# Score sessions of four key-major blocks, PV per 512 queries and V for four head groups at a time, in two sliding-window attention layers

## The chip, the cores and the metric

One core of one Trainium2 chip (not the same chip in every job). The metric is the device time of one execution in microseconds (us); medians of several executions are given with their range. PE is the TensorE matmul engine, DVE is VectorE, ACT is ScalarE, POOL is GpSimd, SP is SyncE, which issues DMAs. The profile comes from one execution; its span is 1 to 2 us shorter than the time of that execution. "Granted clock" is the share of full speed that TensorE was given; in this case's traces it is 1.00 or 0.5, in steps of 3.4 us.

## The reference

Two independent layers A and B, outputs put side by side. Each has 2048 tokens, width 1024, 32 heads of 32 dimensions, and a causal window of 256 keys:

```python
qkv = (x @ wqkv).reshape(B, S, 3, H, Dh)...          # S = 2048, H = 32, Dh = 32
scores = einsum("bhqd,bhkd->bhqk", q, k) * Dh ** -0.5
mask = (i - j >= 0) & (i - j < 256)
p = softmax(where(mask, scores, -1e9))
out = einsum("bhqk,bhkd->bhqd", p, v)...reshape(B, S, D) @ wo
```

In blocks of 128, a query block meets three key blocks, so a head has 45 blocks of scores (16 + 15 + 14). Four heads form a group; two layers of eight groups make 16 groups.

## The kernel before

Matmuls of the projections fill the time in which TensorE would wait for exponentials: a "session" is the scores of one query block, their exp, and then some filler. The tiles that decide what may run ahead:

```python
ps_st   = tile_pool(name="ps_st",   bufs=1, space=PSUM)   # scores st [P, 4, 512] F32
ps_acc  = tile_pool(name="ps_acc",  bufs=1, space=PSUM)   # acc [P, 2, 2, 128] F32: PV | row sums, 256 queries
ps_proj = tile_pool(name="ps_proj", bufs=3, space=PSUM)   # pp, of every projection
```

For each query block i, up to three blocks of scores for each of four heads, and one exp over all of them:

```python
st = ps_st.tile([P, 4, 512], F32, name="st")
for jj in range(nk):                                      # nk = 1, 2, 3, 3, ...
    for r in range(4):                                    # four heads
        nc.tensor.matmul(st[:, r, jj*P:(jj+1)*P], lhsT=kT[...], rhs=qT[..., i*P:(i+1)*P],
                         start=True, stop=True, tile_position=(32*r, 0))
nc.scalar.activation(out=pt[:, :, kb0:kb0+nk, a, :], in_=st[...], func=ACT.Exp, ...)
```

Two query blocks later comes PV (the exponentials times V) with the row sums in the same accumulator, then on DVE two reciprocals and one multiplication into oT. The filler of a group is Q and K (64 matmuls of 512 columns) and V (128 of 128 columns, four blocks in one pp buffer), in the order in which the sessions need them, the same amount in every group:

```python
for g in range(G):
    for i in range(NB):
        emit_proj(inf, g, i // 4)                         # what this session cannot do without
        pt = qk_exp_mask(g, i)
        if i % 2 == 1 and len(pend) >= 2: pvl_pair(*pend.pop(0))
        ...
        emit_proj(max(need_p, budget - need_o), g + 1)    # filler, then the output projection of A
```

Each finished Q or K chunk is cast out of pp by DVE (an eviction: it frees the pp buffer; V and the output are evicted by ACT), which then takes its absolute maximum for a certificate that exp without a running maximum is safe (a slow path exists and is not taken). The certificate's last step is one tiny matmul at the end.

## Time and profile before

| | before |
|---|---|
| time | 664.51 us median of 3 (663.87 to 665.25) |
| PE, DVE, ACT busy | 94%, 67%, 63% of the span |
| chain that ended last | PE 89%, DVE 4%, ACT 2% |
| granted clock | 1.00 until the last slice (no record before 13.9 us) |

The prediction quotes the page's shares and waits. Two more rows of the page: busy tenths of PE, and granted clock, in 40 equal slices (9 is 90% or more). And one group: its columns are line, engine, operation, output and input, count, then busy us and mean ns of one, then idle time before it.

```profile
PE   4999999999999999999999999999999999999996
PEclk9999999999999999999999999999999999999998
...
L260 DVE RECIPROCAL rinv<-acc 128x128 f32<-128x128 f32 x256 | 226.3, 925 | 112.4 <-PE acc L251 111.5
```

There is no slice in which TensorE rests. The reciprocal is DVE's largest group: 256 of 0.925 us.

### The profile page before, as it was taken

Reading aid. Unit: us, or ns where it says so; the run is one execution under the profiler, and the core shown is the slowest. Engines: PE = TensorE matmul, PEld = TensorE weight load, DVE = VectorE, ACT = ScalarE, POOL = GpSimd, SP = SyncE. Lnnn points to the kernel's source line nnn. Section 1 sums busy time; section 2 is a strip of 40 time slices with the busy share of each in tenths; the row PEclk is TensorE's granted clock in tenths of the full one; section 3 lists DMA queues with packets and bytes.
Section 4 is the critical chain, followed back from the end, with each engine's and each line's share of the span. In section 5 each row is a group of like instructions: output and inputs, shape, how many; then the busy total and the mean of one; then the engine's idle time right before and its main releaser. Section 6 shows DMA issues by size and latency. Waiting matters only on the chain.

```text
span 663.4 us, 22408 instructions
## 1 busy us (share of the span) xinstructions
PE 626.1 (94%) x10175; PEld 366.6 (55%) x10308; DVE 444.7 (67%) x677; ACT 418.8 (63%) x385; POOL 294.3 (44%) x487
## 2 busy tenths in 40 slices
PE   4999999999999999999999999999999999999996
PEld 2555666665565655565555555555555555544442
DVE  1688877878788888877676777767676777553000
ACT  0666666576676676667666667666666667775332
POOL 0454545455455555555545455444545445452000
PEclk9999999999999999999999999999999999999998
DMA  9992202022010116102020020202011000011121
GB/s 209 278 253 43 49 2 49 4 48 44 9 42 9 32 28 136 38 3 49 18 65 2 20 64 2 66 18 49 19 31 37 18 2 18 34 49 54 75 80 68
DMA packets 89733, 35.06 MB, mean 53 GB/s; under 512 B 83488, under 2 KB 83488, under 8 KB 89632
## 3 DMA queue, kind: packets, MB, share of 16 engines
q1 hardware_dynamic: 89632, 33.56, 20.7%
q8 instruction: 82, 1.34, 0.9%
q14 instruction: 19, 0.16, 0.1%
HBM read 16.78 MB, written 8.39 MB: 38 GB/s over the span
## 4 chain that ended last, share of the span: by engine, by line
PE 89%; DVE 4%; issue 2%; ACT 2%; SPq 1%; DMA 1%; ACTq 0%; DVEq 0%
PE pp L133 33%; PE pp L151 18%; PE pp L193 16%; PE acc L251 13%; PE st L216 10%; ACT pt L224 2%; DVE rinv L260 2%; DVE pm L139 1%; SPq L82 1%; DMA wst<-in_A_wqkv_dram 1%; DVE oT L261 0%; DVE kT L110 0%; ACT osb L108 0%; DVE qT L110 0%; ACT vt L108 0%
## 5 line engine op out<-in xcount | busy, mean ns | idle before, releaser
L224 ACT ACTIVATE pt<-st 128x1536 bf16<-128x1536 f32 (+2 forms) x256 | 350.9, 1371 | 172.1 <-PE st L216 170.2
L260 DVE RECIPROCAL rinv<-acc 128x128 f32<-128x128 f32 x256 | 226.3, 925 | 112.4 <-PE acc L251 111.5
L228 POOL TENSOR_SCALAR_AFFINE_SELECT pt<-pt 128x512 bf16<-128x512 bf16 x256 | 162.4, 634 | 309.9 <-ACT pt L224 309.9
L133 PE MATMUL pp<-xT,wst 128*128 128x512 bf16 x912 | 234.8, 383 | 20.6 <-issue 10.0
L133 PEld LDWEIGHTS <-wst 128*128 128x128 bf16 x1024 | 87.0, 98 | 102.8 <-issue 14.4
L232 POOL TENSOR_SCALAR_AFFINE_SELECT pt<-pt 128x512 bf16<-128x512 bf16 x224 | 142.1, 634 | 0.0
L151 PE MATMUL pp<-wst,xT 128*128 128x128 bf16 x2048 | 140.4, 220 | 0.7 <-issue 0.5
L151 PEld LDWEIGHTS <-xT 128*128 128x128 bf16 x2048 | 119.6, 98 | 24.1 <-issue 7.4
L193 PE MATMUL pp<-wo_sb,oT 128*128 128x512 bf16 x491 | 127.6, 379 | 3.1 <-issue 1.3
L216 PEld LDWEIGHTS <-kT 32*128 32x128 bf16 x2880 | 44.5, 92 | 94.2 <-issue 89.0
L216 PE MATMUL st<-qT,kT 32*128 32x128 bf16 x2880 | 86.7, 218 | 4.7 <-ACT pt L224 3.6
L193 PEld LDWEIGHTS <-oT 128*128 128x128 bf16 x512 | 47.3, 98 | 50.5 <-issue 1.3
L110 DVE CAST qT<-pp 128x512 bf16<-128x512 f32 x64 | 43.3, 677 | 41.0 <-PE pp L133 37.2
L108 ACT CAST osb<-pp 128x512 bf16<-128x512 f32 x64 | 37.4, 585 | 47.7 <-PE pp L193 46.8
L251 PE MATMUL acc<-pt,vt 128*32 128x256 bf16 (+1 forms) x1920 | 63.3, 249 | 1.9 <-DVE oT L261 1.7
L251 PE MATMUL acc<-pt,ones 128*32 128x256 bf16 (+1 forms) x1920 | 62.3, 246 | 0.0
L261 DVE TENSOR_TENSOR oT<-acc,rinv 128x256 bf16<-128x256 f32 x128 | 53.6, 419 | 2.9
L108 ACT CAST vt<-pp 128x512 bf16<-128x512 f32 x64 | 37.2, 582 | 18.1 <-PE pp L151 17.9
L139 DVE TENSOR_REDUCE pm<-qT 128x1 f32<-128x512 bf16 x64 | 43.8, 684 | 1.7
L139 DVE TENSOR_REDUCE pm<-kT 128x1 f32<-128x512 bf16 x64 | 43.6, 681 | 1.2
L110 DVE CAST kT<-pp 128x512 bf16<-128x512 f32 x64 | 42.2, 660 | 2.6 <-PE pp L133 2.1
L251 PEld LDWEIGHTS <-vt 128*32 128x32 bf16 x1920 | 33.8, 95 | 17.4 <-DVE oT L261 3.4
(20 smaller groups left out, 48.2 us busy)
## 6 DMA issues: line engine op xcount, KB each, us to landing
out_dram<-osb SPq DMA_DIRECT2D x32, 256.0 KB, 2.0
wst<-in_A_wqkv_dram SPq DMA_DIRECT2D x24, 256.0 KB, 4.2
wst<-in_B_wqkv_dram SPq DMA_DIRECT2D x24, 256.0 KB, 4.3
wo_sb<-in_A_wo_dram SPq DMA_DIRECT2D x1, 2048.0 KB, 8.8
wo_sb<-in_B_wo_dram SPq DMA_DIRECT2D x1, 2048.0 KB, 11.0
xT<-in_A_x_dram SPq DMA_TRANSPOSE x4, 7.4
xT<-in_B_x_dram SPq DMA_TRANSPOSE x4, 7.3
```

The costliest lines, as they stand in the source:

```text
L108: nc.scalar.copy(out=out, in_=in_)
L110: nc.vector.tensor_copy(out=out, in_=in_)
L133: nc.tensor.matmul(st_["pp"][:], lhsT=wst[g][:, ct, which, :], rhs=xt[:, ct, o:o + QW], start=(ct == 0), stop=(ct == CT - 1))
L139: nc.vector.tensor_reduce(out=grp[g][3][:, which, sc:sc + 1], in_=dst, axis=AX.X, op=ALU.max, apply_absolute_value=True)
L151: nc.tensor.matmul(st_["pv"][:, a, :], lhsT=xt[:, ct, o:o + P], rhs=wst[g][:, ct, 2, :], start=(ct == 0), stop=(ct == CT - 1))
L193: nc.tensor.matmul(st_["po"][:], lhsT=oTs[pi * T + ct][:, sb * P:(sb + 1) * P], rhs=wo_sb[pi][:, ct, ch * cfg.NW:(ch + 1) * cfg.NW], start ...
L216: nc.tensor.matmul(st[:, r, jj * P:(jj + 1) * P], lhsT=kT[32 * r:32 * r + 32, (j0 + jj) * P:(j0 + jj + 1) * P], rhs=qT[32 * r:32 * r + 32, ...
L224: nc.scalar.activation(out=pt[:, :, kb0:kb0 + nk, a, :], in_=st[:, :, :nk * P].rearrange("p r (j q) -> p r j q", q=P), func=ACT.Exp, bias= ...
L228: nc.gpsimd.affine_select(out=dg, in_=dg, pattern=[[0, 4], [1, P]], compare_op=ALU.is_ge, fill=0.0, base=0, channel_multiplier=-1)
L232: nc.gpsimd.affine_select(out=fb, in_=fb, pattern=[[0, 4], [-1, P]], compare_op=ALU.is_gt, fill=0.0, base=0, channel_multiplier=1)
L251: nc.tensor.matmul(acc[32 * r:32 * r + 32, which, a0:a0 + na, :], lhsT=lhsT, rhs=pt[:, r, kb, a0:a0 + na, :], start=(which == 0 and n == 0 ...
L260: nc.vector.reciprocal(out=rinv[:, a, :], in_=acc[:, 1, a, :])
```

## The change

The intent is fewer and larger pieces: less change between kinds of matmul, fewer instructions, a cheaper certificate, no rest of projection work at the end.

1. **Key-major sessions.** The 45 (key block, query block) pairs are listed key by key and cut into sessions of four: 12 per group instead of 16. One score matmul takes all queries that belong to one key block.
2. **PV per 512 queries**: acc grows to two banks' worth, so pp goes from three buffers to two. Reciprocals and multiplications are queued and issued between filler matmuls.
3. **V for four groups at a time**, 512 columns wide: V is wanted every fourth group only.
4. Filler is a list of chains (matmuls that fill one pp buffer) with earliest and latest sessions, and a session emits the larger of a base and of what the deadlines need.
5. The certificate becomes an in-place OR over the bit patterns; the head loads smaller pieces on two queues and warms TensorE with zero matmuls; the output projection starts right behind the last group.

A session that finds no filler to emit is called dry below.

```diff
+QB = 4
+SLOTS = 4
+NS_BASE = 1750.0
+PV_LAG = 2
...
-    ps_proj = ctx.enter_context(tc.tile_pool(name="ps_proj", bufs=3, space=PSUM))
+    ps_proj = ctx.enter_context(tc.tile_pool(name="ps_proj", bufs=2, space=PSUM))
...
-                        evac(EVAC_QK, dst, st_["pp"][:])
-                        nc.vector.tensor_reduce(out=grp[g][3][:, which, sc:sc + 1], in_=dst,
-                                                axis=AX.X, op=ALU.max, apply_absolute_value=True)
+                    nc.vector.tensor_copy(out=dst, in_=st_["pp"][:])
+                    seen = top[:, which, :].bitcast(I32)
+                    nc.vector.tensor_tensor(out=seen, in0=seen, in1=dst.bitcast(I32),
+                                            op=ALU.bitwise_or)
...
+    for m in range(NPROB * T // SB):                      # SB = 4 groups
+        for b in range(NB):
+            k = b // QB
+            g = m * SB
+            early = NS * (g - 1) if k < 2 else pv_time(g - 1, k - 1) + 1
+            chains.append(_Chain(early, pv_time(g, k), v_steps(m, b)))
...
+    def need(now):
+        rate, work = 0.0, sum(ns for ns, _ in current)
+        for c in chains:
+            if c.late >= 10 ** 6:
+                break
+            work += NS_MM * CT
+            rate = max(rate, work / (c.late - now)) if c.late > now else rate
+        return rate
...
+            for _, f in qk_steps(0, which, 0, lo, hi, held[which], last=(hi == 512)):
...
+        emit(now, max(NS_BASE, need(now)))
```

## The prediction

> **What bounds the kernel now.** I read the engine shares first, then the chain of work that ended last, then the waits, then a stretch of the timeline. From the page, busy time by engine and the chain by engine and by line:
>
> ```profile
> PE 626.1 (94%) x10175; PEld 366.6 (55%) x10308; DVE 444.7 (67%) x677; ACT 418.8 (63%) x385; POOL 294.3 (44%) x487
> ...
> PE 89%; DVE 4%; issue 2%; ACT 2%; SPq 1%; DMA 1%; ACTq 0%; DVEq 0%
> PE pp L133 33%; PE pp L151 18%; PE pp L193 16%; PE acc L251 13%; PE st L216 10%; ACT pt L224 2%; DVE rinv L260 2%; DVE pm L139 1%; SPq L82 1%; DMA wst<-in_A_wqkv_dram 1%; DVE oT L261 0%; DVE kT L110 0%; ACT osb L108 0%; DVE qT L110 0%; ACT vt L108 0%
> ```
>
> TensorE is the bound: 89% of the chain, and all of it in five kinds of matmul: Q/K projection (L133), V projection (L151), output projection (L193), PV with row sums (L251), scores (L216). ACT is 63% busy and DVE 67%, so neither is near its limit on average. The waits say how rarely PE is held up by them (engine and line, released by: us in all, times, longest):
>
> ```profile
> PE st L216 <- ACT pt L224: 3.6, 10, 0.6
> PE acc L251 <- DVE oT L261: 1.7, 4, 0.5
> PE pp L193 <- ACT osb L108: 1.2, 3, 0.4
> ```
>
> That is 6.5 us of 663. Busy time of single matmuls overlaps, so I take PE's cost from start-to-start times in the timeline (start, length, what):
>
> ```profile
> 241.00 2.12 PE L133 MATMUL pp<-xT,wst 128*128 128x512 bf16 x9
> 243.04 0.35 PE L216 MATMUL st<-qT,kT 32*128 32x128 bf16 x12
> 243.32 0.51 PE L251 MATMUL acc<-pt,vt 128*32 128x128 bf16 x16
> 243.66 0.50 PE L251 MATMUL acc<-pt,ones 128*32 128x128 bf16 x16
> ...
> 253.41 1.35 PE L151 MATMUL pp<-wst,xT 128*128 128x128 bf16 x21
> 254.69 0.35 PE L216 MATMUL st<-qT,kT 32*128 32x128 bf16 x12
> ```
>
> Nine 512-wide matmuls and the step into the scores take 2.04 us: 9 x 0.2157 = 1.94, and 0.10 of change. Twelve score matmuls hold PE 0.28 us; elsewhere x8 holds it 0.22 and x4 0.17, so 0.055 us per block of 4 heads and 0.115 fixed. The 16 PV matmuls take 0.34 us: 6 blocks at 0.0556. V's 128-wide matmuls follow each other in 0.056. From the end of row sums to the next full matmul is 0.10.
>
> Sum for before: 1536 wide matmuls x 0.2157 = 331.3; 2048 V x 0.056 = 114.7; scores 16 groups x (16 sessions x 0.215 + 45 blocks x 0.0556) = 95.1; PV 16 x (8 x 0.10 + 90 x 0.0556) = 92.9. That is 634.0. The head is 8.6 us to the first matmul plus 3.4 for 16 matmuls at 0.43 instead of 0.216; the tail after the last projection 6.6; waits about 9. Total 661.6 against the 663.4 profiled. The sum closes, so I trust its terms.
>
> **What the Trainium skill says.** "TensorE: Matmul & The Clock Gate", section "Wait — 56ns, not 53.3ns?", gives 55.6 and 215.7 ns start to start at N = 128 and 512; the trace agrees (0.056, 0.2157). So V in 512-wide matmuls gains only the fixed 2.5 ns per matmul, not a factor. "TensorEngine Tiling (Array Packing)", "Key Properties", says that changing the tiling mode drains TensorE; the trace shows 0.10 to 0.115 us per change. "ScalarE: Activation LUTs", "What ACT_TABLE_LOAD costs", gives an ACTIVATE with immediates as 186 ns + 0.833 ns per element. The exps of three widths agree (us busy, mean ns of one):
>
> ```profile
> L224 ACT ACTIVATE pt<-st 128x1536 bf16<-128x1536 f32 x224 | 324.9, 1450 | 150.2 <-PE st L216 148.3 <-PE pp L151 1.2
> ...
> L224 ACT ACTIVATE pt<-st 128x1024 bf16<-128x1024 f32 x16 | 16.4, 1025 | 12.1 <-PE st L216 12.1
> ...
> L224 ACT ACTIVATE pt<-st 128x512 bf16<-128x512 f32 x16 | 9.6, 598 | 9.7 <-PE st L216 9.7
> ```
>
> Slope (1450 - 598) / 1024 = 0.832; 2048 elements should take 1.876 us. The first page's "What's actually happening" says idle TensorE falls to half clock after some 3.4 us windows; before shows 1.00 from stage to stage, so no run tests it yet.
>
> **The change part by part.** Scores: 12 sessions per group in place of 16 (45 blocks, four to a session, one in the last). 16 x (12 x 0.215 + 45 x 0.0556) = 81.3, saves 13.8. PV: four per group instead of eight, same columns: 16 x (4 x 0.10 + 90 x 0.0556) = 86.5, saves 6.4. V: 512 wide matmuls x 0.2157 = 110.4, saves 4.3. Q/K and output projection keep their 1536. PE's work falls by 24.5 to 609.5 us. Exps: 176 of 1.876 and 16 of 0.598 are 339.8 us, against 350.9: ACT gains little. DVE: casts and reciprocals stay; 128 reductions of 0.68 (87 us) become in-place ORs over 256 words; DVE is no bound. POOL's 480 selects stay.
>
> Head: weights go on ACT's queue instead of behind a 4.1 us transpose issue, the first x piece is half as long, zero matmuls warm the clock. I estimate the first real matmul at 7.5 us, at full clock, but then the second x piece is wanted at about 11 and, 4.1 us of issue plus about 7.4 us to landing behind it, comes at 12 to 14: 2.5 us of wait. Head 10 instead of 12. Tail about 6, as the certificate is computed earlier.
>
> So far 609.5 + 10 + 6 = 625.5 us, 6% faster. **But the filler is uneven.** The score tile st still has one buffer, so a session cannot start before the exp of the one before is done. From score start to exp start is about 0.45 us before, 0.50 with four blocks; with the exp and 0.04 to the next scores, one turn is 2.4 us. PE's own share of it is 0.44, plus 1.43 where a PV falls in it. The rest must be filled with projections, and 9 matmuls (1.94 us, what the base budget of 1750 ns emits) fit just so: 12 x 9 = 108 per group. I counted the list that the diff's emission makes. Q/K of one group is 64 matmuls; V for four groups is 128, and each chain has an earliest session: V may not come before the group ahead of its four. V fills groups 0, 3, 4, 7, 8, 11, 12, the first output projection groups 7 to 9. In groups 2, 5 and 6 only the 64 Q/K matmuls are allowed; they are used up by session 5 or 4, at 9 to 14 a session. Group 14 runs dry at session 8, group 15 has nothing for its first six. Count of dry sessions: 16 full ones without PV, each leaving PE idle 2.4 - 0.44 = 1.95 us, 31.2; 11 with a PV, 0.53 each, 5.8; six short last ones, 0.55 each, 3.3; half-filled ones about 3. **43 us of new wait**, which before spread at 3.6.
>
> Second, acc has one buffer: four reciprocals (about 0.84) and multiplications (0.28, estimated from 0.42 for twice the width) are 4.7 us of DVE per PV, and between the PVs of a dry group's sessions 10 and 1 (the next) there are two full turns and a short one, with PE itself ahead: about 2 us in each of five groups, 10. Third, acc takes two banks and the projection buffers go from three to two. A chain lasts 1.73 us. A V or output eviction can sit behind a whole exp: up to 1.88 + 0.58, 0.7 too late; a Q/K cast behind reciprocal and multiplication: 0.2 + 1.2 + 0.68, 0.35 too late. With roughly a quarter of 256 chains hit at 0.25 on average: 15 us, 5 to 25.
>
> Sum: 625.5 + 43 + 10 + 15 = 693.5. I choose 690 because turns may be a little quicker than I add up.
>
> **The rivals.** One: PE stays the bound, the dry sessions' PVs and scores hide inside exps, and the savings come through: 625 to 645. For it: PE's 89% of the chain now, and ACT's total work falls. Against it: the count of dry sessions follows from the order in the diff, and a single st buffer has no way round. Two: only the dry sessions bite and two projection buffers suffice (each eviction is 0.58 to 0.68 in a chain of 1.73): 668 to 680. For it: before waited 1.2 us for osb. Against: that was with three buffers and exps of 1.45. Three: TensorE, a third busy over some 14 us of dry sessions, is throttled and restarts at half clock: about 1.7 us per dry stretch, and PV inside the turn doubles; 700 to 715. Four: the head waits longer, because 1 MB of V weights and all of x share the DMA engines (already fully busy in the first 33 us): plus 5.
>
> **Range and chances.** Low end: the smallest plausible waits, 35 + 5 + 5, over 622 gives 667; high end: rival three on the sum, 712. Faster by over 2% (under 651) would need under 26 us of waits in all, which the count of dry sessions alone exceeds: 0.10, for an error of kind. Within 2% (651 to 678) 0.19. Slower 0.71.
>
> **What will show it.** Right: exps of 2048 elements near 1.88 us; "PE st waits for ACT pt" rising from 3.6 to some 40 us, bunched in five stretches, where PE's digit in the slices drops to 3 to 6; about 609 us of PE pacing in the dense ones; PE waiting for DVE at acc, and pp for ACT and DVE. Wrong: if PE stays at nine tenths in every slice, my reading of the earliest sessions or of the single buffer failed; if scores of 384 columns or PV of four blocks cost more than 0.0556 per block, the work term failed; if pp waits are near zero, the third term.

## The result, and the profile after

The changed kernel is correct and **slower: 738.91 us** median of 4 (737.43 to 739.41), against 664.88 (663.87 to 665.76) for the kernel before in the same rounds. The ratio is 1.111 (95% interval 1.109 to 1.113).

From the page of the changed kernel, the same rows as before: busy time, slices of PE and of its clock, the chain by engine and by line.

```profile
PE 646.8 (88%) x6877; PEld 295.7 (40%) x6877; DVE 449.9 (61%) x776; ACT 410.0 (56%) x321; POOL 301.5 (41%) x484
...
PE   5999999589997867689999998997999998748996
...
PEclk8999999899999979699999999999999999868999
...
PE 66%; DVE 22%; ACT 8%; DMA 2%; issue 1%; SPq 0%; ACTq 0%
```

PE has holes now, in slices 8 (5), 13 to 17 (7, 8, 6, 7, 6), 28 (7) and 34 to 36 (8, 7, 4), and its clock falls in or next to most of these places. In the chain, TensorE lost 23 points, and **DVE rose from 4% to 22%**, although DVE as a whole is less busy than before (61% against 67%). The waits of TensorE (engine and line, what ended the wait: us in all, times, longest):

```profile
PE st L272 <- ACT pt L280: 40.4, 29, 2.1
PE acc L311 <- DVE oT L322: 14.5, 7, 3.5
PE pp L142 <- DMA xT<-in_A_x_dram: 7.1, 2, 5.6
PE pp L142 <- DVE kT L146: 6.9, 9, 1.4
PE pp L142 <- DVE qT L146: 2.8, 7, 1.0
```

The first line is the wait of scores for the exp before them: 3.6 us before, 40.4 now, and 43 were predicted. The second is PV waiting for the normalising of the PV before: 1.7 before. The costs of single instructions that matter:

```profile
L280 ACT ACTIVATE pt<-st 128x2048 bf16<-128x2048 f32 x176 | 330.4, 1877 | 214.4 <-PE st L272 206.3 <-POOL pt L285 4.4 <-POOL pt L289 2.6
L321 DVE RECIPROCAL rinv<-acc 128x128 f32<-128x128 f32 x256 | 243.1, 950 | 170.7 <-PE acc L311 170.7
L148 DVE TENSOR_TENSOR top<-top,kT 128x256 int32<-128x256 int32 x64 | 33.3, 520 | 2.2
```

The exp is as predicted to the nanosecond (1.876). Now a dry stretch in the timeline of TensorE (start, length, line, what, count, in brackets the idle time before and what ended it):

```profile
252.18 0.40 PE L272 MATMUL st<-qT,kT 32*128 32x384 bf16 x8 [1.07 <-ACT pt L280]
254.64 0.60 PE L272 MATMUL st<-qT,kT 32*128 32x256 bf16 x8 [2.06 <-ACT pt L280]
255.17 1.47 PE L311 MATMUL acc<-pt,vt 128*32 128x128 bf16 x28
256.42 1.50 PE L311 MATMUL acc<-pt,ones 128*32 128x128 bf16 x28
...
267.73 5.17 PE L142 MATMUL pp<-xT,wqk 128*128 128x512 bf16 x14
```

From scores to scores one dry turn is 254.64 - 252.18 = 2.46 us, of which the exp takes 1.88 and the scores and the two hand-overs the rest. Then the second thing: the same 28 PV matmuls that hold TensorE for 0.67 us at full clock (from 182.75 to 183.42 us, start to start) hold it 1.25 here, and 14 projections take 5.17 us where 12 take 2.76 at full clock (from 143.55 us). TensorE has fallen to half clock. In all, 76.7 us of the span run at half clock, nearly all in dry stretches and in the head.

And a crowded stretch, on DVE, where only Q and K chains are left as filler:

```profile
84.94 0.96 DVE L321 RECIPROCAL rinv<-acc 128x128 f32<-128x128 f32 x1 [0.38 <-PE acc L311]
85.93 0.29 DVE L322 TENSOR_TENSOR oT<-acc,rinv 128x128 bf16<-128x128 f32 x1
86.14 0.95 DVE L321 RECIPROCAL rinv<-acc 128x128 f32<-128x128 f32 x1
87.12 0.29 DVE L322 TENSOR_TENSOR oT<-acc,rinv 128x128 bf16<-128x128 f32 x1
87.33 0.68 DVE L146 CAST qT<-pp 128x512 bf16<-128x512 f32 x1
88.05 0.42 DVE L148 TENSOR_TENSOR top<-top,qT 128x256 int32<-128x256 int32 x1
88.39 0.95 DVE L321 RECIPROCAL rinv<-acc 128x128 f32<-128x128 f32 x1
```

DVE has no pause. Casts, ORs and reciprocals stand in one queue, and a cast behind which a pp buffer comes free finds up to 1.2 us of other work ahead of it.

Last, the head:

```profile
7.37 1.91 PE L142 MATMUL pp<-xT,wqk 128*128 128x256 bf16 x16 [1.44 <-DMA xT<-in_A_x_dram]
14.91 3.57 PE L142 MATMUL pp<-xT,wqk 128*128 128x256 bf16 x16 [5.64 <-DMA xT<-in_A_x_dram]
```

The first matmul of the projections comes at 7.37 us (7.5 was predicted), but the second piece of x lets TensorE wait 5.64 us, and the clock is down by then. First scores come at 19.27 us; before they came at 16.55.

### The profile page after: what moved, and what is told of

Its sections match the earlier page's. It is cut to its first block, busy times and chain, and to the rows that moved or that the text cites. A ratio compares the mean times of both kernels' runs of the same rounds, so it can differ in the third digit from the quotient of the medians.

```text
span 737.6 us, 15737 instructions
## 1 busy us (share of the span) xinstructions
PE 646.8 (88%) x6877; PEld 295.7 (40%) x6877; DVE 449.9 (61%) x776; ACT 410.0 (56%) x321; POOL 301.5 (41%) x484
## 4 chain that ended last, share of the span: by engine, by line
PE 66%; DVE 22%; ACT 8%; DMA 2%; issue 1%; SPq 0%; ACTq 0%
PE pp L142 17%; PE pp L181 15%; PE pp L164 14%; PE acc L311 13%; DVE rinv L321 11%; PE st L272 7%; ACT pt L280 7%; DVE oT L322 4%; DVE qT L146 3%; DVE kT L146 2%; DVE top L148 2%; DMA xT<-in_A_x_dram 2%; ACT vt L167 0%; ACT osb L185 0%; SPq L94 0%
## 5 line engine op out<-in xcount | busy, mean ns | idle before, releaser
L280 ACT ACTIVATE pt<-st 128x2048 bf16<-128x2048 f32 x192 | 340.0, 1771 | 234.5 <-PE st L272 226.4
L142 PE MATMUL pp<-xT,wqk 128*128 128x512 bf16 (+1 forms) x1040 | 251.1, 386 | 17.5 <-DMA xT<-in_A_x_dram 7.1
L142 PEld LDWEIGHTS <-wqk 128*128 128x128 bf16 x1040 | 96.2, 100 | 136.9 <-issue 44.6
L164 PE MATMUL pp<-wv,xT 128*128 128x512 bf16 x512 | 121.6, 380 | 3.6 <-DVE kT L146 1.7
L272 PE MATMUL st<-qT,kT 32*128 32x256 bf16 (+2 forms) x1472 | 77.1, 281 | 44.7 <-ACT pt L280 40.4
L322 DVE TENSOR_TENSOR oT<-acc,rinv 128x128 bf16<-128x128 f32 x256 | 74.5, 291 | 8.8
L164 PEld LDWEIGHTS <-xT 128*128 128x128 bf16 x512 | 46.6, 98 | 63.5 <-issue 14.1
L311 PE MATMUL acc<-pt,vt 128*32 128x256 bf16 (+2 forms) x1664 | 57.2, 280 | 14.5 <-DVE oT L322 14.5
L311 PE MATMUL acc<-pt,ones 128*32 128x256 bf16 (+2 forms) x1664 | 58.2, 283 | 0.0
L311 PEld LDWEIGHTS <-ones 128*32 128x32 bf16 x1664 | 40.1, 107 | 6.5 <-issue 1.3
```

What stands on the lines that cost most here:

```text
L142: nc.tensor.matmul(st_["pp"][:, lo:hi], lhsT=w_, rhs=xT[(pi, k)][:, ct, lo:hi], start=(ct == 0), stop=(ct == CT - 1))
L164: nc.tensor.matmul(st_["pp"][:], lhsT=xT[(pi, k)][:, ct, a * P:(a + 1) * P], rhs=wv[m][:, ct, :], start=(ct == 0), stop=(ct == CT - 1))
L272: nc.tensor.matmul(st[:, r, a * P:b * P], lhsT=kT[32 * r:32 * r + 32, j * P:(j + 1) * P], rhs=qT[32 * r:32 * r + 32, q0 * P:(q0 + b - a) * P],
L280: nc.scalar.activation(out=pt[:, :, :n, :].rearrange("p r j q -> p r (j q)"), in_=st[:, :, :n * P], func=ACT.Exp, bias=-SHIFT, scale=cfg.s ...
L311: nc.tensor.matmul(acc[32 * r:32 * r + 32, which, o:o + n * P], lhsT=lhsT, rhs=pts[(g, s)][:, r, a:a + n, :], start=(x == 0), stop=(x == l ...
L322: nc.vector.tensor_tensor(out=oTs[(pi, k)][:, t, sl], in0=acc[:, 0, sl], in1=rinv[:, sl], op=ALU.mult)
```

## The experiments

Twelve kernels, all correct. Where one time is given it is one execution; four executions of the changed kernel spread over 2 us. The kernel before stood at 664.16 to 664.90 us in those jobs, with a range within 1.3 us to either side. Edits are shortened. The theories: **clock** (half clock after dry sessions is the part that the prediction left out), **uneven filler** (V in blocks of four groups, spent too early, leaves some groups dry and others crowded), **DVE's order** (in crowded groups evictions stand behind other DVE work), and **buffers** (two pp buffers and one acc are too few).

### Zero matmuls in the dry sessions

```diff
-        emit(now, max(NS_BASE, need(now)))
+        done = emit(now, max(NS_BASE, need(now)))
+        idle = (1950.0 if full_session else 500.0) - done - (1430.0 if pv_in_it else 0.0)
+        if idle > 2 * NS_MM and not current:
+            fill = ps_proj.tile([P, 512], F32, name="pp")
+            for _ in range(int(idle / NS_MM)): nc.tensor.matmul(fill[:], lhsT=zt[:, 0:P], rhs=zt[:], ...)
```

> The changed kernel with zero matmuls that nobody reads added on TensorE in the sessions that have no projections left (as many as fit into the wait for the exp: up to 9, or 2 where a PV falls in). Clock theory: the low granted clock of the dry stretches (0.6 to 0.9 there, 0.948 in all) is caused by TensorE idling in them and costs about 30 us; with the added work the clock is 0.98 or more and the time falls from 739 to 705-718, though work was added. Rival (the low clock only marks idle time and costs nothing; DVE and ACT waits are the whole loss): 737 or more.

Measured: 731.91 us, mean granted clock 0.981 instead of 0.948. The wait for exponentials became work on zeros:

```profile
PE acc L311 <- DVE oT L322: 14.9, 7, 3.5
...
PE st L272 <- ACT pt L280: 4.0, 13, 0.6
```

By start-to-start times the loss to half clock fell from 25 to 8 us, but the time fell by 7 only. The time lies between the theory's (705 to 718) and the rival's (737 or more): the clock theory is right about the pace and wrong about the size. The timelines show why. A dry turn without PV takes 2.46 us in both kernels. One with a PV takes 3.22 us in the changed kernel (scores at 254.64, next ones at 257.86) and 2.45 here (256.10 to 258.55). The PV of that turn takes 1.26 us longer at half clock (255.17 to 257.86, against 256.43 to 257.86), so 0.77 of it lengthens the turn and the rest is time that TensorE would have waited anyway.

### Pacing by what can start, with a smaller base

```diff
-NS_BASE = 1750.0
+NS_BASE = 1250.0
...
+            if c.early > now:
+                continue
             work += NS_MM * CT
```

> The changed kernel, but the emission looks only at chains that may start now, and the base budget is 1250: the same projections are spread at 6 to 8 per session through the poor groups, so no session before the last group is dry, while the idle in sum stays (waits of the scores for the exp about 42 by my count of the order, 46 as it was). Clock theory: clock 0.98 or more and 739 falls by about 30 to 705-715. Rival (the waits are the loss, not the clock): 730 to 739.

Measured: 733.53 us, clock 0.984. The dry sessions are gone as such, but the wait is now spread: 37.1 us in 64 pieces instead of 40.4 in 29, and 22.6 us at acc. Again the clock came back and 5 us with it, as the rival said (730 to 739). But 5 us is a net figure: the waits of scores for DVE's casts rose from 4.1 to 14.1 us and those at acc by 8.1. The filler itself was too lumpy for this pacing rule to smooth.

### V for two groups at a time

```diff
-    SB = 512 // P
+    SB = 256 // P
...
-                nc.tensor.matmul(st_["pp"][:], lhsT=xT[...], rhs=wv[m][:, ct, :], ...)   # 512 columns, one block
+                    nc.tensor.matmul(st_["pp"][:, h, :], lhsT=xT[...], rhs=wv[m][:, ct, :], ...)   # 256 columns, two blocks
```

> The changed kernel with V for two groups at a time (256 columns) instead of four, the emission as it was. If V in fours is what makes the filler uneven: fewer dry sessions (groups 4, 6 and 15 still have some), waits of scores for exps from 40 to about 26, and 739 falls by 18 (waits alone) to 35 (with the clock): 704-721. Rival (V in fours is harmless, its 128-wide form would be no better): 735 or more, and V matmuls of 256 columns should cost 0.109 each.

Measured: 715.38 us, clock 0.964, waits for exponentials 25.8 us, at acc 6.6. This is 23.5 us off, as expected, by changing how many groups one block of V serves, with the same multiplications. (The edit, here and wherever V's width changes, also loads V's weights earlier and into more buffers. In the changed kernel's view of waits TensorE never waits for them, so that is not the gain.)

### V for two groups, and pacing with the old base

```diff
 (the edit above, and)
+            if c.early > now:
+                continue
```

> V for two groups and the emission that looks only at chains that may start now, base budget 1750: by my count no dry session before group 15. Theory (uneven filler with one score buffer is the loss, clock included): waits of scores for exps about 12, clock 0.98, time about 667-675. Rival (buffers acc and pp are the larger loss): 700 or more.

Measured: **682.32 us**, clock 0.982. Far more than the two edits alone (5 and 23.5, the first with a smaller base): pacing helps once there is something in every group to pace. The expectation (667 to 675) was missed by 7 us, and so was the rival's. What TensorE still waited for:

```profile
PE st L276 <- ACT pt L284: 6.6, 5, 2.1
...
PE pp L142 <- DVE kT L146: 4.7, 6, 1.4
```

The waits left are mostly for DVE's evictions.

### PV per 256 queries again, and three pp buffers

```diff
-    ps_proj = ... bufs=2
+    ps_proj = ... bufs=3
...
-        acc = ps_acc.tile([P, 2, 512], F32, name="acc")
+        acc = ps_acc.tile([P, 2, PQ * P], F32, name="acc")       # PQ = 2: 256 queries
```

> The changed kernel with PV and row sums per 256 queries again (accumulator one bank instead of two, so three projection buffers instead of two), all else as changed. Theory (the 512-query accumulator costs more through the buffers than its fewer starts save): waits of projection matmuls for DVE and ACT, some 22 us by start-to-start count, fall to the few us of the head; acc waits from 15 to under 5; PV pays about 6 us for twice as many starts; 739 falls to 712-722. Rival (these waits only stand in for the dry sessions and move into the scores' wait): 732 or more, with the scores' wait for the exp rising by as much.

Measured: 751.01 us, so worse, and outside both expectations: the rival had the scores' wait rise, and it fell from 40.4 to 30.4. pp waits for evictions vanish, and PV waits take their place: 41.4 us in 41 pieces (14.5 in 7 before this edit). The clock is lower too, 0.925. My reading: a third pp buffer does not help while the same DVE has to free acc twice as often. It is argued, since the edit changes acc and pp together. Nor is a 256-query acc bad in itself: the kernel before has one and waited 1.7 us for it, with its PVs evenly spaced (243.32, 247.95, 252.64 us).

### The loads of the head in another order

```diff
-    load_wv(0, nc.scalar, parts=2)
+    load_wv(0, nc.sync)
...
-    load_wqk(0, nc.scalar, halves=(1,))
+    load_wqk(0, nc.sync, halves=(1,))
```

> The changed kernel with the V weights and the second half of the first Q/K weights behind the x pieces on one queue, instead of beside them on ACT's. Theory (weights sharing the DMA engines hold back the second x piece, which landed at 14.9 us): it lands by 10-11, the first exp starts 3 to 6 us earlier than 19.7, and the time falls by as much, 733-736. Rival (the transposes alone take that long): no change, 738-739.

Measured: 738.61 us, no difference. The first scores came at 11.96 instead of 19.27, and the next projection then waited 4.19 us for the next piece of x, and ran at half clock. Whatever TensorE does first, it waits for the next bytes of x.

### All of these at once

Edits of the four sections above, and the certificate's matmul put some chains later.

> V for two groups, emission by what may start now, PV per 256 queries with three projection buffers, the head of the run above, and the certificate's matmul two chains later than its DVE part. If the causes add up: 682 of the run with the first two, less about 18 of buffer waits, 4 of head, 3 of the certificate, plus 6 for PV starts: 655-668, at or below the kernel before (664). Rival (the waits only trade places): 675 or more.

Measured: 714.19 us (713.43 to 715.40), ratio to before 1.0745 (1.0721 to 1.0768). This is a miss, and a useful one: 32 us worse than V for two groups with pacing. Of the three edits that were added, the small acc is the one that shows: TensorE waits 45.8 us, 54 times, for it. Here two PVs can come 3.5 us apart (254.99 and 258.51).

### The OR out of the way of evictions

In the crowded stretch each cast is followed at once by its OR, and the next cast or reciprocal waits for that. Here the OR joins the queue of normalising steps, and is issued after at least 700 ns of further filler. Same instructions, same result:

```diff
-                    seen = top[:, which, :].bitcast(I32)
-                    nc.vector.tensor_tensor(out=seen, in0=seen, in1=dst.bitcast(I32), op=ALU.bitwise_or)
+                    def seen_or(dst=dst):
+                        seen = top[:, which, :].bitcast(I32)
+                        nc.vector.tensor_tensor(out=seen, in0=seen, in1=dst.bitcast(I32), op=ALU.bitwise_or)
+                    side.append(seen_or)
```

> The changed kernel with one thing moved: the certificate's OR of a finished Q or K chunk is no longer issued on VectorE straight behind the eviction, but put into the queue of normalising steps and issued after at least 700 ns of further filler matmuls. Same instructions, same sizes, same result. Theory VectorE's order: in the crowded groups an eviction waits behind the OR of the chain before, and a PV waits behind evictions and ORs, so the projections' waits for evictions fall by some 10 us or more and the time to 717 to 727. Rival, the waits are set by the score buffer and by the clock alone: 735 or more, the same waits.

Measured: 726.85 us, 12 us off, with clock (0.944) and waits for exponentials unchanged. What fell is DVE's part:

```profile
PE st L272 <- ACT pt L280: 40.7, 29, 2.1
PE acc L311 <- DVE oT L322: 8.1, 5, 2.5
...
PE pp L142 <- DVE kT L146: 2.7, 5, 0.7
```

The time is right at the edge of the expectation (717 to 727). DVE was busy for as long as before, even a little longer (the ORs took 0.56 us each instead of 0.51), so it was its order, not its load, that held TensorE. One thing more moved with the edit: it empties the queue before the certificate. In the changed kernel the certificate's three DVE steps (2.05 us of work, from 648.04) stand before three reciprocals that the next PV needs, and that PV waits 3.5 us, the longest wait at acc; here this wait is gone, but the certificate's own matmul waits 5.1 us instead of 2.0. The two nearly cancel.

### The same in the evenly filled kernel

Edit: V for two groups, pacing, the OR late, the certificate's matmul later.

> The even-filler kernel of before (V for two groups at a time, turns paced by the chains that can start) with the OR moved in the same way and the certificate's one matmul put later. It was 682.3. Theory: 660 to 671, because the waits for evictions of Q and K were what was left. Rival: within 3 us of 680.

Measured: 668.36 us, 14 us under the 682.32. As expected. Up to 4 us of it may be the certificate's: its matmul had waited 3.9 us for DVE in the kernel without these edits.

### Everything that the theory asks for

V for one group at a time, four blocks to one pp buffer, as the kernel before had it; pacing by what can start, with base 1900; OR once per two chunks and late; normalising steps at least 900 ns of filler apart; the certificate's matmul later.

```diff
-    SB = 512 // P
+    SB = 128 // P
...
-            if side and since >= 700.0:
+            if side and since >= 900.0:
...
+                    if k % 2:
+                        side.append(seen_or)                     # 512 int32 elements at once
```

> Everything that the theory asks for: V for one group at a time (four blocks in one projection buffer), turns paced by the chains that can start with a base of 1900 ns, the OR once per two chunks and late, normalising steps no closer than 900 ns of filler apart so that an eviction gets in between, the certificate's matmul later. Theory: waits only for scores behind exponentials (12 us) and the head, 649 to 660, faster than the kernel before. Rival, single score and pair of projection buffers cost more than the order can give back: 665 to 680.

Measured: **654.11 us** (652.76 to 654.93), ratio to before 0.983 (0.981 to 0.984): 1.7% faster than the kernel before, and by the medians 11.5% faster than the changed one. Its PE row, its clock and its waits:

```profile
PE   5999999999999999899999999999999999969996
...
PEclk9899999999999999999999999999999999969999
```

```profile
PE st L277 <- ACT pt L285: 6.9, 4, 2.1
PE pp L142 <- DMA xT<-in_A_x_dram: 4.6, 2, 3.4
...
PE acc L316 <- DVE oT L327: 0.7, 1, 0.7
```

The holes are gone but for one at 573 to 584 us, where the last V is done and the output projection may not yet start, and the clock is low there. Waits for DVE's casts are at about 1 us a line. (The view's first line, left out here, is 8.8 us of "issue", in 55 pieces of 0.2 us at most.) With the same two pp buffers, the same single acc and the same single score buffer as in the changed kernel, TensorE hardly waits for pp and acc, and for the exp 6.9 us instead of 40.4.

### The same with the head's loads reordered

Edit: as in the head experiment, on the kernel of 654.11.

> The fastest kernel so far (654.1) with the loads of the head in another order: the first V weights and the second half of the first Q and K weights behind the first x pieces in one queue, instead of beside them in another. In an earlier run that had V weights in this order among other things the first scores came at 13.7 us, here they come at 16.4. Theory: now that no later wait absorbs it, the 2.7 us reach the end, 650.5 to 652.5. Rival: as in the changed kernel itself, where the same edit gave nothing, within 1 us of 654.

Measured: 653.64 us (651.95 to 654.92), ratio to before 0.984 (0.982 to 0.986): the rival was right. The first scores did come 2.7 us earlier, at 13.71, and the next piece of x took it back:

```profile
23.43 0.82 PE L142 MATMUL pp<-xT,wqk 128*128 128x512 bf16 x3 [2.42 <-DMA xT<-in_A_x_dram]
```

### The same with V for four groups again

Edit: the kernel of 654.11, with V as in the change (`SB = 512 // P`, one buffer for its weights, loaded as there), all else kept.

> The fastest kernel so far with one thing taken back: V for four groups at a time, as in the change, everything else kept (turns paced by availability with a base of 1900 ns, late OR, spaced normalising steps, late certificate matmul). Theory: the width of the V block decides how even the filler is, sessions without filler and groups crowded with Q and K come back whatever the pacing, 685 to 702, with waits for exponentials near 25 us and for the normalising near 25 us. Rival, the pacing and VectorE's order were the whole matter: 653 to 665.

Measured: **703.15 us**, 49 us worse, with clock 0.956 and the old waits:

```profile
PE st L275 <- ACT pt L283: 23.9, 18, 2.1
PE acc L314 <- DVE oT L325: 15.7, 17, 2.6
```

So this one choice, V for four groups at a time, costs 49 us in this kernel, twice the 24.5 us of TensorE's work that the prediction saw the whole change save. A slightly worse value than expected (685 to 702), and far from the rival's (653 to 665). Not tested: V for four groups with earlier starts and more vt buffers. What is shown is that V in these lumps costs so much, not that its width does.

## Why the prediction was right and wrong

**Right: the direction, and the mechanism behind most of it.** The prediction counted 33 dry sessions and 43 us of new wait for exponentials; the view of waits has 29 and 40.4. One dry turn was put at 2.4 us and takes 2.46. The exp was 1.876 and is 1.877, the first matmul 7.5 and 7.37. That the filler is uneven because V comes every fourth group, and that this outweighs all the savings, is what the runs with V for two groups and with V for four groups again showed, from either side. Where the filler is even, the kernel with sessions of four blocks and 512-query PV beats the kernel before; no run separates these savings from those of the cheaper certificate and the new head.

**Wrong: the size, by 49 us, and the range.** The prediction's terms were start-to-start times, so I read the changed kernel in the same way (an own reading of its trace, good to some us a line; each start-to-start time is split into work at full pace, loss to half clock, and wait). These waits come out longer than in the view, because a matmul's modelled end lies after the moment at which the next could have started.

| term, us | predicted | measured |
|---|---|---|
| work at full pace, and lead-in to the first matmul | 617.0 | 611.6 |
| head: wait for the second x piece | 2.5 | 5.6 |
| wait before scores | 43 | 51.4 |
| wait before PV | 10 | 15.4 |
| wait before projections, without the head's | 15 | 22.4 |
| loss to half clock | 0 | 24.7 |
| tail | 6 | 6.5 |
| sum | 693.5 | 737.6 |

(617.0 is 609.5 plus 7.5.) Another 3.5 us were lost by rounding 693.5 down to 690, for "turns may be a little quicker than I add up", where they were slower; and 1.3 us lie between the profile's span and the time.

Three steps failed:

- **"Rival three ... about 1.7 us per dry stretch" was left out of the sum.** The trace has the half clock that this rival described, and 24.7 us of it instead of some 1.7 for each of five stretches. But its price is not its size: both runs that brought the clock back, with zero matmuls and with a smaller base, gained only 7 and 5 us, net of what their edits cost. The prediction held that no run had tested the half clock yet; but the "0.43 instead of 0.216" of its own head term is half pace, in a stretch for which the trace before holds no record of the clock (the record begins at 13.9 us).
- **"DVE is no bound", with no price on the ORs.** DVE was judged by its average of 67%. The ORs take 0.51 us each, 65.6 in all, straight behind the casts, where the next eviction and the next reciprocal wait for them. Moving them alone out of the way gave 12 us. The reciprocals are not what failed: "four reciprocals (about 0.84)" is too short (the page of the kernel before already had 925 ns, the changed kernel has 950), but 4 x (0.84 + 0.28) is 4.5, and the sum used 4.7 us per PV; a reciprocal and its multiplication take 1.19 us from start to start, so 4.76.
- **"A quarter of 256 chains hit at 0.25 on average"** sized the third term as if lateness were spread evenly. It is bunched where only Q and K chains are left, each of which needs a cast and an OR while the normalising of a PV goes on: 22.4 us instead of 15. The two pp buffers that the term blamed are not enough to cause it: with two and an even filler almost no such wait remained (654). Three were only tried together with a smaller acc, where the wait moved to acc (751).

How much each is worth can only be estimated. I replayed the order of emission with single buffers and durations from the trace, without any clock effect: with 0.84 for a reciprocal and 0.35 for an OR, 711 us; with the measured 0.95 and 0.51, 732. This tells how sensitive the order is to DVE's durations (21 us), not how large the error was, as the sum used neither 0.84 nor 0.35. A second replay gives 17 us for the same step, 16 for taking the ORs away and 13 for moving them (12 measured). It falls 20 to 26 us short of the profiled span in the six runs with 512-query PV and a clock of 0.98 or more, and 37 short in the changed kernel; by that the half clock costs the changed kernel 11 to 17 us. (It fits the two runs with 256-query PV less well, 34 and 55 short.)

The half clock's net 7, the ORs' 12 and the 4.8 of rounding and span are shown, each by a run or a figure. The other half of the 49 is argued: more of the half clock and of the ORs, and waits that the averages made too small. The head's longer wait is real, but loading in another order, which shortened its first part, gave nothing in two kernels. The sum for the kernel before closed with "waits about 9", of which its view of waits shows 7.

On rival two, the answer is no for this kernel: its projections waited some 15 us for evictions by the view of waits. In the evenly filled kernel with the new order on DVE, the two buffers do suffice.

## What to carry to other kernels

Before making one kind of filler wider, list how much filler each stage has and from when it may be spent: filler that arrives in lumps leaves later stages dry, and pacing can't mend what isn't there. Price an engine at its crowded place, instruction by instruction in queue order, not by its average, and put work that nobody waits for (a certificate, a statistic) behind the work that frees a buffer. A clock that falls in idle stretches was here mostly a symptom: fill the stretch, and expect less back than the lost pace adds up to.

## What the Trainium skill lacked or had wrong

- "GPSIMD Engine Reference", section "1. Specifications", says that GpSimd's SBUF interfaces are shared with VectorE and that VectorE instructions with two SBUF inputs contend; that section gives no size. The OR has two SBUF inputs, and the changed kernel's trace agrees: 53 ORs with no select running on POOL took 0.425 us on average, 44 that lay wholly beside selects 0.604, the longest OR 0.902. Reciprocals, which read PSUM, took 0.949 and 0.947.
- "VectorE: DVE Perf Modes", section "The TRN2 errata", gives (N + 151) / 0.96 ns for an fp32 two-tensor add. For the 256 int32 elements of the OR that is an estimate of 424 ns, and the shortest OR took 424: the page had what the prediction needed. But neither that section nor another of the page gives a time for the reciprocal, which was DVE's largest group: 0.950 us for 128 elements.
- "TensorE: Matmul & The Clock Gate", section "HAM oscillation", gives the rule that TensorE must have no idle gap over about 3.4 us. That rule is not enough here. Between the head and the tail of the changed kernel no gap in the 3.4 us before a fall of the clock was longer than 3.0 us, and the clock still halved, for 3.4, 6.8 or 10.2 us at a time. It is the busy share of the 3.4 us window that shows: before each fall TensorE was busy for at most 0.43 of the window (for 0.45 us in the one before the fall at 254.7 us), and no window at full clock with 0.50 or more was followed by a fall.
- No page says what half clock costs when the stretch is waiting anyway: 17 us of regained pace were worth 7 us of time in the run with zero matmuls.
